# Key features of a polynomial-sketch attention: sums left in PSUM for the first factor, products from PSUM and SBUF by group of tiles

## The chip, the cores and the metric

The kernel runs on one core of one Trainium2 chip. The metric is device time in microseconds (us), the median of repeated runs; 425.93 us before the change. A profile of one execution gives the times of the single instructions. The engines are TensorE (PE, with its weight loads as PEld), VectorE (DVE), ScalarE (ACT), GpSimd (POOL) and SyncE (SP, which issues DMAs).

## What is computed

Two blocks one after the other. The first is an attention without softmax. Each query and key vector is projected twice, and the outer product of the two projections is its feature vector; the second is a sum over four experts, each a two-layer MLP. Cut to what matters:

```python
def phi(x):                                  # x: (4, 4, 1088, 32), S1, S2: (8, 32)
    a = np.einsum('rd,bhsd->bhsr', S1, x)    # first factor, 8 numbers
    b = np.einsum('rd,bhsd->bhsr', S2, x)    # second factor, 8 numbers
    return np.einsum('bhsi,bhsj->bhsij', a, b).reshape(*x.shape[:-1], 64)
q_p, k_p = (phi(q), phi(k))
kv = np.einsum('bhsf,bhsd->bhfd', k_p, v)
z = np.sum(k_p, axis=2)
num = np.einsum('bhsf,bhfd->bhsd', q_p, kv)
den = np.einsum('bhsf,bhf->bhs', q_p, z)[..., None] + 1e-06
x = (num / den)                              # laid out as 4352 tokens of 128
p = domain_probs / (domain_probs.sum(-1, keepdims=True) + 1e-09)
for e in range(4):                           # w1: (4, 128, 1024), w2: (4, 1024, 128)
    out += p[:, e:e + 1] * (np.maximum(x @ w1[e], 0.0) @ w2[e])
```

S1 and S2 come as float64. The kernel writes each of their numbers as a float32 and a smaller rest, so a projection is a product with the high part plus a product with the low part.

## The kernel before

**The main loop.** The MLP takes the tokens in ten chunks of 128 to 512 and, for each chunk and expert, the hidden units in eight blocks of 128. One pass of the loop at line 1468 is one such block (a slot; the first chunk, of 128 tokens, takes two blocks a slot). A block of the usual kind (`opening`, line 1094) takes one PSUM bank `g`, and PE multiplies two of three weight parts into it (`h<-xs,wa` and `h<-xs,wb`); ACT scales the bank in place (L1135). One slot later `third` (line 1154) adds the third part (`h<-xs,wd`) and has the engines make three operands out of the bank: ACT `ha` (L1184) and for some blocks `hc` (L1186), DVE `hb` (L1191) and for some `hc` (L1206), POOL others (L1213, L1214). Some slots later `second` (line 1220) multiplies these by the second layer (`o<-ha,va`, `o<-hb,vb`, `o<-hc,vd`). So each block of this kind has one `wa` matmul and one `hb`, and both come in the order of the blocks. `MAKERS` says by a letter which engine makes what for each block.

**The banks.** Six of the eight PSUM banks serve the tag `h`. Their owner is decided when the program is written out, by a queue (lines 123 to 137): `psum` takes the bank at the head of `spare`, `given_back` puts one at its tail. A block's bank is given back in `third`, that is one slot after it was taken. A matmul into a bank waits on the chip until the last reader of the bank's previous content has finished.

**The attention as pieces.** The attention of batches 1 to 3 is written as generators (`keys`, `queries`), and each `yield` ends a piece. The loop deals the pieces among the slots (`work`, line 1483): a credit grows by a rate that follows how many pieces the next chunk still needs, and a piece is written out while there is credit and the estimated DVE time `vector_time` is under `LIMIT` (1300 ns). `on_vector` (line 1407) adds elements/0.96 + 80 ns for each DVE instruction, and each slot takes off 1600 ns for a chunk of 512 tokens (1400 for 448). Batch 0 goes another way (`start`, line 966), which the change leaves alone.

**The keys of one batch.** 1088 keys of four heads are nine tiles of 128 (the last is half full), in groups of 4, 4 and 1 (`FG`, line 449). The tile `kp` holds the transposed keys (from its column 1024) and later the features. In `keys` (line 562):

- three pieces transpose the keys on DVE;
- `key_project_wide` (line 491) takes a bank `kf`, makes one matmul per tile, 128 columns each (64 of the high part of S, then 64 of the low part; each 64 are 4 heads by 16, 8 first factors and 8 second), and ACT copies the high half into the SBUF tile `fs` (this copy has L51 in the profile, the helper's line);
- `key_add` (line 504) adds the low half, from PSUM, to `fs`, on DVE, in place; the bank is given back, before the next group takes its own;
- `key_product_wide` (line 519) multiplies first and second factors out of `fs`, both operands in SBUF, into `kp`: four instructions, tiles 0 to 3 and 4 to 8, for each of two pairs of heads (p), with an empty piece after each;
- the queries are turned, and 80 small matmuls (L318) sum the features times the values and project the queries.

Up to the turn of the queries that makes three pieces of transposes, three of projections (the last two with an add) and eight of products, the first of which has the third add.

Of the kernel before, what the change touches and what calls it, by code (L numbers as in the profile page):

```python
# [12 lines left out]
ALU = mybir.AluOpType  # L13
# [4 lines left out]
def _ap(t, p0: int, np_: int, off: int, free):  # L18

    p = list(t.ap)[0]  # L20
    return bass.AP(t.tensor, t.offset + p0 * p[0] + off, [[p[0], np_]] + [list(d) for d in free])
# [3 lines left out]
def kernel(  # L25
# [24 lines left out]
    nc = tc.nc  # L50
    scalar_copy = lambda to, of: nc.scalar.activation(to, of, ACTF.Copy)  # L51

    P = 128
    HP = 64
    B, H, S, D = q.shape
    E, DM, F = w1.shape
    R = 8
    R2 = 2 * R
    G = S // 32
    assert (B, H, S, D) == (4, 4, 1088, 32) and (E, DM, F) == (4, P, 1024)  # L60
    NT = 9
# [56 lines left out]
    ps_h = ctx.enter_context(tc.tile_pool(name="ps_h", bufs=1, space=bass.MemoryType.PSUM))  # L118
# [6 lines left out]
    def psum(pool, tag):  # L125
        if pool is not ps_h:
            return pool.tile([P, 512], F32, tag=tag, name=tag)
        bank = spare.pop(0)
        t = pool.tile([P, 512], F32, tag=f"h{bank}", name="h")
        home[t.tensor.name] = bank  # L130
        return t

    def given_back(t):

        bank = home.pop(t.tensor.name, None)
        if bank is not None:
            spare.append(bank)
# [12 lines left out]
    def load_q(b):  # L150
        qn[b] = lpool.tile([P, S], F32, tag="rows", name="qn")
        load_rows(q, b, qn[b])
# [104 lines left out]
    sk = cpool.tile([P, P], F32, name="sk")  # L257
# [5 lines left out]
    kTs, kps = {}, {}  # L263

    def key_tiles(b):
        t = apool.tile([P, NT * 2 * P], F32, tag="kp", name="kp")
        kps[b] = t[:, :].rearrange("p (t i f) -> p t i f", i=2, f=P)
        kTs[b] = t[:, NT * P - P :]
        nc.gpsimd.memset(kTs[b][:, S : P * NT], 0.0)
# [179 lines left out]
    FG = ((0, 4), (4, 4), (8, 1))  # L449
    fss, kvzs, kvx = {}, {}, {}  # L450

    def key_turn(b, r, t0=0, n=4):
        if r < 2:
            nc.vector.transpose(
                _ap(kTs[b], 0, P, 512 * r + P * t0, [[P, n], [32, 4], [1, 32]]),
                _ap(kn[b], 0, P, P * r + 32 * t0, [[32, n], [8 * D, 4], [1, 32]]),
            )
        else:
            nc.vector.transpose(kTs[b][:, 1024:S], kn[b][:, 1024:S])

    def value_copy(b):
        if b:
            return
        for r in range(2):
            scalar_copy(
                vx[:, 4 * r : 4 * r + 4, :, 0:D].rearrange("p t h d -> p h t d"),
                _ap(vn[b][r], 0, P, 0, [[4 * D, H], [D, 4], [1, D]]),
            )
            yield
        scalar_copy(vx[0:64, 8, :, 0:D], _ap(vn[b][2], 0, 64, 0, [[D, H], [1, D]]))  # L470
# [20 lines left out]
    def key_project_wide(b, gi, kf):  # L491

        t0, n = FG[gi]
        if gi == 0:
            fss[b] = apool.tile([P, 2, NT, 32], F32, tag="fs", name="fs")
        for t in range(n):
            nc.tensor.matmul(  # L497
                kf[:, P * t : P * t + P], kTs[b][:, P * (t0 + t) : P * (t0 + t + 1)], sk[:, :], start=True, stop=True
            )
        scalar_copy(  # L500
            _ap(fss[b], 0, P, 32 * t0, [[32 * NT, 2], [32, n], [1, 32]]), _ap(kf, 0, P, 0, [[32, 2], [P, n], [1, 32]])
        )

    def key_add(b, gi, kf):
        t0, n = FG[gi]
        fs = _ap(fss[b], 0, P, 32 * t0, [[32 * NT, 2], [32, n], [1, 32]])
        nc.vector.tensor_tensor(out=fs, in0=_ap(kf, 0, P, HP, [[32, 2], [P, n], [1, 32]]), in1=fs, op=ALU.add)

    def key_product(b, t0, n, p, x, eng, kf=None):

# [5 lines left out]
            op=ALU.mult,  # L516
        )

    def key_product_wide(b, t0, n, p):

        nc.vector.tensor_tensor(
            out=_ap(kps[b], 0, P, 256 * t0 + P * p, [[256, n], [HP, 2], [1, HP]]),
            in0=_ap(fss[b], 0, P, 32 * (NT * p + t0), [[32, n], [R2, 2], [1, R], [0, R]]),
            in1=_ap(fss[b], 0, P, 32 * (NT * p + t0) + R, [[32, n], [R2, 2], [0, R], [1, R]]),
            op=ALU.mult,
        )

    def key_sum(b, p, kv, t0=0, n=NT):
        for t in range(t0, t0 + n):
            both(  # L530
                kv[:, 256 * p : 256 * p + 2 * (D + 1)],
                kps[b][:, t, p, :],
                vx[:, t, 2 * p : 2 * p + 2].rearrange("p h d -> p (h d)"),

                start=(p == t == 0),
                stop=(t == NT - 1),
                skip_group_check=True,
            )
# [13 lines left out]
    def key_blocks(b, kv):  # L552

        kvx[b] = apool.tile([P, 2, 2 * (D + 1)], F32, tag="kvx", name="kvx")
        nc.vector.tensor_tensor(
            out=_ap(kvx[b], 0, P, 0, [[2 * (D + 1), 2], [D + 1, 2], [1, D + 1]]),
            in0=_ap(kv, 0, P, 0, [[256, 2], [D + 1, 2], [1, D + 1]]),
            in1=_ap(own_half if b else own2, 0, P, 0, [[0, 2], [1, 2], [0, D + 1]]),
            op=ALU.mult,
        )  # L560

    def keys(b):
        key_tiles(b)
        for r in range(3):
            key_turn(b, r)
            yield
        load_q(b)
        kf = []
        for gi in range(3):
            if gi:  # L570
                key_add(b, gi - 1, kf[gi - 1])
                given_back(kf[gi - 1])
            kf.append(psum(ps_h, "h") if gi == 1 else psum(ps_h, "h"))
            key_project_wide(b, gi, kf[gi])
            yield
        key_add(b, 2, kf[2])
        given_back(kf[2])
        for _ in value_copy(b):
            yield
        for t0, n in ((0, 4), (4, 5)):  # L580
            for p in range(2):
                key_product_wide(b, t0, n, p)
                yield
                yield
        first = UNITS[b][0]
        turned[b, 0] = query_turn(b, 0, first)
        yield
        yield
        kv = psum(ps_h, "h")
        for p in range(2):  # L590
            key_sum(b, p, kv)
        project(b, 0, first)
        yield
        key_blocks(b, kv)
        given_back(kv)
        yield
        store_rows(b, 0, first)
        if SPREAD:
            spread(b, 0, first)
        yield  # L600
# [29 lines left out]
    def query_turn(b, c, n):  # L630
        qT = apool.tile([P, QW], F32, tag="qT", name="qT")
        for _ in query_turns(b, c, n, qT):
            pass
        return qT
# [140 lines left out]
    def project(b, c, n):  # L775

        qT = turned[b, c]
        qc, w = psum(ps_h, "h"), n // 2
        for i in range(2):
            for _ in range(2):  # L780
                on_side(
                    lambda s: qc[half[s], 0:w],
                    lambda s: sq_half[:, i, :],
                    lambda s: qT[:, w * s : w * s + w],
                    start=(i == 0),
                    stop=(i == 1),
                )
        scalar_copy(qT[:, 0:w], qc[:, 0:w])
        given_back(qc)
# [3 lines left out]
    def store_rows(b, c, n):  # L793

        qT, w = turned.pop((b, c)), n // 2
        rows = rows_of_unit[b, c] = dram.tile([HP, n], F32, name=f"rows_{b}_{c}")
        for s in range(2):
            nc.sync.dma_start(rows[:, w * s : w * s + w], qT[half[s], 0:w])
        if SPREAD == 0:
            spread(b, c, n)  # L800

    def spread(b, c, n):

        rows = rows_of_unit.pop((b, c))
        t = fetched[b, c] = apool.tile([P, 4, QW], F32, tag="kp", name="qs")
        for p in range(2):
            at = rows.offset + R2 * p * n
            nc.sync.dma_start(t[:, p, 0:n], bass.AP(rows.tensor, at, [[n, R2], [0, R], [1, n]]))
            for i in range(2):
                nc.sync.dma_start(  # L810
                    t[half[i], 2 + p, 0:n], bass.AP(rows.tensor, at + (32 + R * i) * n, [[0, R], [n, R], [1, n]])
                )
# [220 lines left out]
    def front():  # L1033
        for b in range(B):
            if b:
                yield from keys(b)
                if b + 1 < B:
                    load_v(b + 1)
            c = 0
            for n in UNITS[b]:  # L1040
                if b or c:
                    yield from queries(b, c, n)
                c += n
# [424 lines left out]
    while i < len(slots) or i <= max(due) or owed:  # L1468
        vector_time[0] = max(0.0, vector_time[0] - (SLOT * CHUNKS[slots[i][1]] / CW if i >= first_slot[1] and i < len(slots) else 900.0))
        scalar_time[0] = max(0.0, scalar_time[0] - (SLOT_A * CHUNKS[slots[i][1]] / CW if i >= first_slot[1] and i < len(slots) else 900.0))  # L1470
        if i < len(slots):
            kind, m, _, _ = slots[i]
# [101 lines left out]
```

## Time and profile before

| | |
|---|---|
| three runs | 425.80, 425.93, 425.94 us |
| median | 425.93 us |
| the profiled execution, its own time | 426.43 us |
| its span from first to last instruction | 424.7 us |
| granted TensorE clock | 1.00 |
| DVE busy in 54 to 60, 70 to 76 us | 5.97, 5.90 of 6 us |
| ACT busy in 148 to 154, 154 to 160 us | 6.00, 4.46 of 6 us |
| key projections (L497), three batches | 54 matmuls, 272/275/275 ns |
| ACT copies into `fs`, all batches | 12, 211/384/477 ns |

Triples are shortest, median and longest. In a row of a profile, `kp<-fs` is what is written and what is read, by the program's names; `x12` is a count; an entry in brackets is the time that the engine stood idle before the row, and what ended it. A row's duration runs from its start to its end, and rows of one engine overlap a little. L numbers are lines of the kernel. "Busy" counts the time in which at least one instruction was under way.

### The profile page before, as it was taken

To read this page: it belongs to the slowest core of one execution; us is meant where nothing else is said; L and a number is where in the kernel's file an instruction comes from. 1 tells how busy PE (TensorE), PEld (TensorE's weight loads), DVE (VectorE), ACT (ScalarE), POOL (GpSimd) and SP (SyncE) were. 2 spreads that over 40 slices of the span, in tenths; PEclk is the share of its full clock that TensorE was granted. 3 is DMA by queue.
4 is the path that set the end of the run, shared out by engine and by line. 5 is a ranking of instruction groups with operands and counts; after the bars stand their busy time and mean duration, and the time that the engine had idled before them with its cause. 6 is when DMAs were issued, how large, how long until landed. Compare 5 with 4: busy or idle time off the path is not lost.

```text
span 424.7 us, 8812 instructions
## 1 busy us (share of the span) xinstructions
PE 416.5 (98%) x2819; PEld 351.7 (83%) x2819; DVE 357.0 (84%) x626; ACT 382.0 (90%) x818; POOL 355.3 (84%) x371
## 2 busy tenths in 40 slices
PE   9999999999999999999999999999999999999996
PEld 7886677888888887878888887878778888989995
DVE  5869999888798896898799996896897878879894
ACT  4368898999999998999999988998999999999992
POOL 6441468999999999997999998897989999799992
PEclk9999999999999999999999999999999999999999
DMA  6925250446512401643602415212621221040110
GB/s 194 320 60 130 47 145 2 98 80 158 165 40 51 126 27 44 136 99 95 176 5 61 114 26 117 61 33 62 161 32 23 41 75 35 23 82 27 34 38 19
DMA packets 57646, 34.66 MB, mean 82 GB/s; under 512 B 34945, under 2 KB 50689, under 8 KB 57601
## 3 DMA queue, kind: packets, MB, share of 16 engines
q1 hardware_dynamic: 57504, 34.01, 31.5%
q8 instruction: 22, 0.36, 0.4%
q14 instruction: 24, 0.19, 0.2%
q10 hardware_dynamic: 96, 0.10, 0.1%
HBM read 28.94 MB, written 5.15 MB: 80 GB/s over the span
## 4 chain that ended last, share of the span: by engine, by line
PE 82%; ACT 8%; DVE 4%; issue 3%; DMA 2%; SPq 0%; DVEq 0%; ACTq 0%
PE o L949 36%; PE h L949 36%; PE h L318 6%; ACT ha L1184 3%; ACT h L1135 3%; ACT hc L1186 2%; PE h L497 1%; DMA qn_first<-in_q_dram 1%; PE o L318 1%; DMA kn<-in_k_dram 1%; PE h L1121 1%; DVE hb L1191 1%; DVE o L1396 1%; SPq L171 0%; DVE qs L637 0%
## 5 line engine op out<-in xcount | busy, mean ns | idle before, releaser
L1214 POOL TENSOR_TENSOR hc<-hb,hc 128x512 fp32r<-128x512 f32 (+3 forms) x204 | 252.5, 1260 | 23.1 <-DVE hb L1191 16.9
L1191 DVE SCALAR_TENSOR_TENSOR hb<-h,ha 128x512 fp32r<-128x512 f32 (+3 forms) x266 | 166.8, 641 | 48.9 <-ACT hc L1186 16.9
L1135 ACT ACTIVATE h<-h 128x512 f32<-128x512 f32 (+3 forms) x283 | 166.3, 588 | 4.1 <-PE h L949 3.5
L1184 ACT ACTIVATE ha<-h 128x512 fp32r<-128x512 f32 (+3 forms) x252 | 148.8, 590 | 2.0 <-PE h L949 0.4
L949 PE MATMUL h<-xs,wd 128*128 128x512 f32 (+3 forms) x283 | 109.2, 386 | 1.3 <-ACT h L1135 0.5
L949 PE MATMUL h<-xs,wa 128*128 128x512 f32 (+3 forms) x283 | 105.5, 373 | 0.0
L949 PE MATMUL h<-xs,wb 128*128 128x512 f32 (+3 forms) x283 | 102.5, 362 | 0.0
L949 PE MATMUL o<-ha,va 128*128 128x512 f32 (+3 forms) x266 | 96.8, 364 | 1.1 <-DVE total L1397 1.1
L949 PE MATMUL o<-hb,vb 128*128 128x512 f32 (+3 forms) x266 | 96.6, 363 | 0.0
L949 PE MATMUL o<-hc,vd 128*128 128x512 f32 (+3 forms) x262 | 79.7, 366 | 0.2
L1186 ACT ACTIVATE hc<-h 128x512 fp32r<-128x512 f32 (+3 forms) x124 | 74.1, 598 | 0.0
L949 PEld LDWEIGHTS h<-xs,wd 128*128 128x128 f32 x283 | 53.3, 188 | 19.8 <-ACT h L1135 11.6
L1213 POOL TENSOR_SCALAR hc<-ha 128x512 fp32r<-128x512 f32 (+3 forms) x80 | 57.4, 717 | 8.1 <-ACT ha L1184 1.6
L949 PEld LDWEIGHTS h<-xs,wa 128*128 128x128 f32 x283 | 53.5, 189 | 9.5 <-issue 2.9
L949 PEld LDWEIGHTS h<-xs,wb 128*128 128x128 f32 x283 | 53.5, 189 | 5.7 <-issue 0.6
L949 PEld LDWEIGHTS o<-ha,va 128*128 128x128 f32 x266 | 50.3, 189 | 7.5 <-PE h L949 2.3
L949 PEld LDWEIGHTS o<-hc,vd 128*128 128x128 f32 x262 | 48.5, 189 | 7.9 <-issue 1.6
L949 PEld LDWEIGHTS o<-hb,vb 128*128 128x128 f32 x266 | 50.3, 189 | 5.5 <-DVE hb L1191 0.2
L1193 DVE SCALAR_TENSOR_TENSOR hc<-ha,hb 128x512 fp32r<-128x512 f32 (+2 forms) x41 | 36.2, 882 | 1.4
L1268 ACT ACTIVATE o<-o 128x512 f32<-128x512 f32 (+3 forms) x33 | 18.4, 557 | 0.0
L1397 DVE TENSOR_TENSOR total<-o,total 128x512 f32<-128x512 f32 (+3 forms) x26 | 16.9, 650 | 0.9
L1396 DVE TENSOR_TENSOR o<-o,gate 128x512 f32<-128x512 f32 (+3 forms) x26 | 16.8, 647 | 0.3 <-PE o L949 0.3
(161 smaller groups left out, 405.2 us busy)
## 6 DMA issues: line engine op xcount, KB each, us to landing
w_sb<-in_moe_w_dram SPq DMA_DIRECT2D x8, 512.0 KB
gate<-gates SPq DMA_DIRECT2D x16, 256.0 KB
kn<-in_k_dram SPq DMA_DIRECT2D x4, 544.0 KB
gate<-gates SPq DMA_DIRECT2D x8, 224.0 KB
qs<-rows SPq DMA_DIRECT2D x6, 288.0 KB
qs<-rows SPq DMA_DIRECT2D x12, 144.0 KB
qn<-in_q_dram SPq DMA_DIRECT2D x3, 544.0 KB
vx<-in_v_dram SPq DMA_DIRECT2D x48, 32.0 KB
```

What stands on the lines that cost most here:

```text
L318: nc.tensor.matmul(out(s), weights(s), moving(s), **flags)
L949: nc.tensor.matmul(to, weights, t, **flags)
L1135: nc.scalar.activation(g, g, ACTF.Copy, scale=1.0 + R12)
L1184: nc.scalar.activation(ha, g, ACTF.Relu, scale=NEAR)
L1186: nc.scalar.activation(hc, g, ACTF.Relu, scale=NEAR * R12)
L1191: nc.vector.scalar_tensor_tensor(out=hb, in0=g, scalar=0.0, in1=high, op0=ALU.max, op1=ALU.subtract)
L1193: nc.vector.scalar_tensor_tensor(out=hc, in0=high, scalar=-R12, in1=rest, op0=ALU.mult, op1=ALU.add)
L1213: nc.gpsimd.tensor_scalar(out=hc, in0=high, scalar1=R12, scalar2=1.0, op0=ALU.mult, op1=ALU.mult)
L1214: nc.gpsimd.tensor_tensor(out=hc, in0=rest, in1=both_, op=ALU.subtract)
L1268: nc.scalar.activation(o[:, 0:n], o[:, 0:n], ACTF.Copy, scale=1.0 + R12)
L1396: nc.vector.tensor_tensor(out=o[:, 0:n], in0=o[:, 0:n], in1=g, op=ALU.mult)
L1397: nc.vector.tensor_tensor(out=total[m][:, 0:n], in0=o[:, 0:n], in1=total[m][:, 0:n], op=ALU.add)
```

## The change

The matmul of the key projection writes its 128 columns as four strips of 32, one for each half of S and pair of heads, so that the bank holds the group by strip, then tile. The ACT copy of the high half follows that layout. `key_add` becomes two instructions of half the size: the first factors' sum is written back into the bank, the second factors' sum into `fs` as before. `key_product_wide` takes a group in place of a range of tiles and reads the first factor from the bank and the second from `fs`: six instructions a batch, for groups of 4, 4 and 1 tiles. In `keys`, the next group's bank is taken and its projection written out ahead of the add of the group before; that group's two products follow in pieces of their own, and its bank is given back after the second. The first product of a group is a piece after its add. The number of pieces up to the turn of the queries stays: three of transposes and eleven behind them.

```diff
--- before.py
+++ after.py
@@ -495,16 +495,24 @@
             fss[b] = apool.tile([P, 2, NT, 32], F32, tag="fs", name="fs")
         for t in range(n):
             nc.tensor.matmul(
-                kf[:, P * t : P * t + P], kTs[b][:, P * (t0 + t) : P * (t0 + t + 1)], sk[:, :], start=True, stop=True
+                _ap(kf, 0, P, 32 * t, [[P, 4], [1, 32]]),
+                kTs[b][:, P * (t0 + t) : P * (t0 + t + 1)],
+                sk[:, :].rearrange("p (a c) -> p a c", c=32),
+                start=True,
+                stop=True,
             )
         scalar_copy(
-            _ap(fss[b], 0, P, 32 * t0, [[32 * NT, 2], [32, n], [1, 32]]), _ap(kf, 0, P, 0, [[32, 2], [P, n], [1, 32]])
+            _ap(fss[b], 0, P, 32 * t0, [[32 * NT, 2], [1, 32 * n]]), _ap(kf, 0, P, 0, [[P, 2], [1, 32 * n]])
         )
 
     def key_add(b, gi, kf):
         t0, n = FG[gi]
-        fs = _ap(fss[b], 0, P, 32 * t0, [[32 * NT, 2], [32, n], [1, 32]])
-        nc.vector.tensor_tensor(out=fs, in0=_ap(kf, 0, P, HP, [[32, 2], [P, n], [1, 32]]), in1=fs, op=ALU.add)
+        of_fs, of_kf = [[32 * NT, 2], [R2, 2 * n], [1, R]], [[P, 2], [R2, 2 * n], [1, R]]
+        nc.vector.tensor_tensor(
+            out=_ap(kf, 0, P, 0, of_kf), in0=_ap(kf, 0, P, 2 * P, of_kf), in1=_ap(fss[b], 0, P, 32 * t0, of_fs), op=ALU.add
+        )
+        fs = _ap(fss[b], 0, P, 32 * t0 + R, of_fs)
+        nc.vector.tensor_tensor(out=fs, in0=_ap(kf, 0, P, 2 * P + R, of_kf), in1=fs, op=ALU.add)
 
     def key_product(b, t0, n, p, x, eng, kf=None):
 
@@ -516,11 +524,12 @@
             op=ALU.mult,
         )
 
-    def key_product_wide(b, t0, n, p):
-
+    def key_product_wide(b, gi, kf, p):
+
+        t0, n = FG[gi]
         nc.vector.tensor_tensor(
             out=_ap(kps[b], 0, P, 256 * t0 + P * p, [[256, n], [HP, 2], [1, HP]]),
-            in0=_ap(fss[b], 0, P, 32 * (NT * p + t0), [[32, n], [R2, 2], [1, R], [0, R]]),
+            in0=_ap(kf, 0, P, P * p, [[32, n], [R2, 2], [1, R], [0, R]]),
             in1=_ap(fss[b], 0, P, 32 * (NT * p + t0) + R, [[32, n], [R2, 2], [0, R], [1, R]]),
             op=ALU.mult,
         )
@@ -567,21 +576,25 @@
         load_q(b)
         kf = []
         for gi in range(3):
+            kf.append(psum(ps_h, "h"))
+            key_project_wide(b, gi, kf[gi])
             if gi:
                 key_add(b, gi - 1, kf[gi - 1])
-                given_back(kf[gi - 1])
-            kf.append(psum(ps_h, "h") if gi == 1 else psum(ps_h, "h"))
-            key_project_wide(b, gi, kf[gi])
+                yield
+                for p in range(2):
+                    key_product_wide(b, gi - 1, kf[gi - 1], p)
+                    if p:
+                        given_back(kf[gi - 1])
+                    yield
+            else:
+                yield
+        key_add(b, 2, kf[2])
+        yield
+        for p in range(2):
+            key_product_wide(b, 2, kf[2], p)
+        given_back(kf[2])
+        for _ in range(3):
             yield
-        key_add(b, 2, kf[2])
-        given_back(kf[2])
-        for _ in value_copy(b):
-            yield
-        for t0, n in ((0, 4), (4, 5)):
-            for p in range(2):
-                key_product_wide(b, t0, n, p)
-                yield
-                yield
         first = UNITS[b][0]
         turned[b, 0] = query_turn(b, 0, first)
         yield
```

`value_copy` yields nothing for the batches that come this way.

## What was predicted

> **What bounds the kernel now.** I read the page's busy times and chain first, then the chain of waits in order of time and the busy times by stretch around the three places where the changed code runs, then the DVE groups by shape, and last the rows in order of time.
>
> ```profile
> PE 416.5 (98%) x2819; PEld 351.7 (83%) x2819; DVE 357.0 (84%) x626; ACT 382.0 (90%) x818; POOL 355.3 (84%) x371
> PE 82%; ACT 8%; DVE 4%; issue 3%; DMA 2%; SPq 0%; DVEq 0%; ACTq 0%
> ```
>
> TensorE (PE) holds 82% of the chain that ended last. VectorE (DVE) is busy 84% of the span but has 4% of that chain. What a DVE saving is worth is therefore decided in the three stretches where `keys` runs (batch 1 near 55 to 70 us, batch 2 near 139 to 156, batch 3 near 232 to 250):
>
> ```profile
> core 0: us, PE busy (x) PEld busy (x) DVE busy (x) ACT busy (x) POOL busy (x), PEclk, DMA share, GB/s
> 60.00:70.00 10.00, 9.31 (x44) 7.37 (x42) 9.89 (x16) 9.93 (x22) 9.33 (x8) 1.00 0.10 23
> 142.00:148.00 6.00, 6.00 (x31) 5.28 (x30) 4.17 (x9) 5.71 (x13) 5.67 (x6) 1.00 0.53 137
> 236.00:242.00 6.00, 6.00 (x31) 5.28 (x30) 5.25 (x10) 5.97 (x13) 5.43 (x6) 1.00 0.73 177
> ```
>
> In batches 2 and 3 PE has no gap, and in the chain by time its matmuls follow at 0.215 us each from 132 to 166 us and from 226 to 260 us. Nothing can be gained there. Every wait that PE is given is added to the end. In batch 1, from 60.1 to 69.8 us, the chain runs through ScalarE (ACT) and "issue"; ACT is busy 9.93 of 10 us and DVE 9.89.
>
> **Part 1, the DVE work.** The durations:
>
> ```profile
> L521 DVE TENSOR_TENSOR kp<-fs 128x640 f32<-128x640 f32 x6 | 7.1, 1191 | 0.0
> L521 DVE TENSOR_TENSOR kp<-fs 128x512 f32<-128x512 f32 x6 | 5.7, 949 | 0.0
> L507 DVE TENSOR_TENSOR fs<-h,fs 128x256 f32<-128x256 f32 x6 | 2.5, 412 | 0.0
> L507 DVE TENSOR_TENSOR fs<-h,fs 128x64 f32<-128x64 f32 x3 | 0.7, 218 | 0.0
> L1396 DVE TENSOR_TENSOR o<-o,gate 128x512 f32<-128x512 f32 x18 | 12.4, 687 | 0.0
> L726 DVE TENSOR_TENSOR xs<-h,rc 128x128 f32<-128x128 f32 x5 | 1.4, 280 | 0.0
> ...
> L521 DVE TENSOR_TENSOR kp<-fs x12: 681/998/1802, 59.4 to 248.8; 128x512 f32<-128x512 f32 x6, 128x640 f32<-128x640 f32 x6
> ```
>
> The old product (two SBUF operands) takes anything from 681 to 1802 ns. The operations with one PSUM operand hardly spread. The new product of four tiles is 512 elements, one PSUM and one SBUF operand: 687 ns by L1396. That of one tile is 128 elements: 280 ns by L726. The repeated operand costs nothing extra: L512 in the first batch has the same pattern and gives 419 ns for 256 elements against L507's 412. The sums are split in two of half the size. From L507's two rows, (412-218)/192 = 1.01 ns an element, so 128 elements are 283 ns and 32 are 186 ns. Writing the sum to PSUM is not dearer: L1396 writes PSUM too.
>
> Per batch, before: adds 2x0.412+0.218 = 1.04 us, products 2x0.949+2x1.191 = 4.28, together 5.32 us in 7 instructions. After: adds 4x0.283+2x0.186 = 1.50, products 4x0.687+2x0.280 = 3.31, together 4.81 us in 12. That is 0.5 us less a batch, 1.5 us less in all. Bounds: if no old product had been held up (0.68 and 0.81 us, the least seen of each shape) the old sum would be 4.0 and the new one costs 0.8 more a batch; if all were like the worst, 2.5 us less. I take the means. On the end this is worth 0 in batches 2 and 3, since PE is the chain there, and I take 0 in batch 1, since ACT is. The cover in batch 1 is thin, and what it is worth if it is gone is the rival on the fast side.
>
> [...]
>
> **Part 2, the key projection and its copy.** Each of the 54 matmuls of L497 (275 ns) writes four strips of 32 columns in place of 128 in a row. In the first batch the projection already writes strips of 32, and the sums of products write 66 columns in a row:
>
> ```profile
> L318 PE MATMUL h<-vx,kp x288: 220/222/272, 9.3 to 254.5; 128*64 128x66 f32 x144
> L318 PE MATMUL h<-sk,kp x72: 222/222/334, 5.8 to 8.0; 128*64 128x64 f32 x72
> ```
>
> Both have 222 ns, so 0. The ACT copy moves as many elements in longer runs: 0, covered on ACT in batches 2 and 3 by PE being the chain. The third group's projection (0.22 us of PE in the chain) and its copy (0.22 us of ACT) move some blocks later. In batch 1 that takes 0.22 us out of a stretch that PE sets (to 59.8 us) and puts the copy into the one that ACT sets: net 0.
>
> **Part 3, the planner.** Per batch `vector_time` now sees 2x427 + 2x(613+613) + 227 + 427 = 3960 ns, where it saw 347+347+147+613+613+747+747 = 3561 (elements/0.96 plus 80 each). Against `LIMIT` I find no piece of batches 2 and 3 pushed to another block: the old products start at 145.74, 148.57, 151.77 and 154.96 us, one in two blocks of some 1.5 us, as their two yields say, so one piece runs in a block and the new ones do too. In batch 1 the third piece reaches 740+613 = 1353, over 1300, and the following four run one to three blocks late. Nothing waits for them before the sums of products at 72.4 us. No DMA is issued elsewhere.
>
> **Part 4, the banks.** This is what I expect to decide. The six `h` banks go round in a queue, and a block of the MLP takes one. With no other user a block reopens the bank of the sixth block before it; each bank that the keys hold shortens that by one. Before, a key bank was back at the next piece. Now group 0's is held over three pieces, group 1's is taken while it is out, and group 2's while group 1's is. At one place in each batch a block then gets the bank of the third block before it. Its first matmul (`h<-xs,wa`) must wait for the last reader of that bank, VectorE's `hb` or `hc`. One `wa` and one `hb` row belong to each block, in the same order, which gives these pairs:
>
> ```profile
> 145.00 0.69 DVE L1191 SCALAR_TENSOR_TENSOR hb<-h,ha 128x512 fp32r<-128x512 f32 x1 [0.97 <-ACT hc L1186]
> 145.35 0.38 PE L949 MATMUL h<-xs,wa 128*128 128x512 f32 x1
> ...
> 238.81 0.68 DVE L1206 SCALAR_TENSOR_TENSOR hc<-h,hid 128x512 fp32r<-128x512 f32 x1
> 238.95 0.38 PE L949 MATMUL h<-xs,wa 128*128 128x512 f32 x1
> ...
> 61.76 0.35 PE L949 MATMUL h<-xs,wa 128*128 128x448 f32 x1
> 62.34 1.26 DVE L1191 SCALAR_TENSOR_TENSOR hb<-h,ha 128x448 fp32r<-128x448 f32 x2
> 62.83 0.55 ACT L1135 ACTIVATE h<-h 128x448 f32<-128x448 f32 x1
> ```
>
> Batch 2: the reader ends at 145.69, the matmul began at 145.35; 0.34 us, and 0.05 for the signal (an L1135 ends at 54.86 and the weight load that it frees starts at 54.91): 0.39 us. This reader waited for ACT, so no lighter DVE brings it forward. Batch 3: 239.49 less 238.95, 0.54, plus 0.07 for DVE having one product more ahead and 0.05: 0.66 us. Batch 1: the first of the two `hb` ends at 62.97, 1.21 us after 61.76; DVE has two adds less ahead of it by then and may end 0.4 sooner, so PE waits 0.8. PE was ahead of ACT there: its second matmul, over at 62.30, would be over at 63.10, and ACT wanted it at 62.83. 0.3 us of that shows. The block after each takes group 0's own bank, free soon after its second product, and the others have 0.4 to 2 us left: 0. What is queued behind the waiting matmul is all of PE; ACT waits next.
>
> Bounds: 0 for each, if the reader comes earlier by as much as PE waits; 0.7 (batch 2, hit at two blocks), 1.2 (batch 3, likewise) and 1.2 (batch 1, all of it) on the other side. I take 0.39 + 0.66 + 0.3 = 1.35 us.
>
> **Sum.** The profiled execution has 426.43 us for its span of 424.7, 1.73 around it; 424.7 + 1.35 + 1.73 = 427.78. It lies 0.50 above the median, 425.93, which is what I count from: 425.93 + 1.35 = **427.3 us**, for this case alone 426.6 to 428.2.
>
> **Rivals.** I call 0.2%, 0.85 us, the least that a measurement of this kernel tells from no change: 426.8 and 425.1 are the borders.
>
> *The waits vanish* (chance 0.26): the readers come some tenths earlier because no product of 1.2 to 1.8 us stands in DVE's queue. For it: batch 2's wait is only 0.39, and DVE idles 0.97 us just before. Against: that reader and batch 3's come before the first long product. Half the waits or less, 426.2 us.
>
> *Faster, the one on the other side* (0.12): in batch 1 it is DVE, not ACT, that sets 60 to 70 us. Its products there took 0.68, 1.27, 0.81 and 1.80 us, with 1.05 of adds 5.61; the new set is 4.81, and twelve rows overlapping by 0.06 each in place of seven (59.36 to 59.96 for a row of 0.68) give 0.3 more: 1.1 us, and 424.8. It decides if the waits of that stretch end on DVE (idle 0.11 of its 10 us) and not on ACT (idle 0.07); the chain names ACT, which speaks against.
>
> *Dependencies* (0.10): ACT's copy of a later group into `fs` waits for the products that still read `fs`, or the third projection waits for products into `kp`, which lie in the same tile. About 1 us a batch on top of the banks: 430.0. Against: in the first batch projections start at 5.8 us while the last transpose into `kp` starts at 6.5, so parts of a tile are told apart.
>
> *Strips cost* (0.02): if four strips doubled the key matmuls, 2.0 us of PE a batch in the chain would be added three times: 425.9 + 1.35 + 6.0 = 433.3. Both 222 ns rows speak against. [...]
>
> **The numbers.** 0.50 for the forecast, 0.26, 0.12, 0.10 and 0.02 for the rivals. Slower by over 0.2%: nearly all of the forecast and the last two, 0.60; within: 0.28; faster: 0.12. The range, 425.2 to 429.2, leaves out most of the fast case and of the dependencies.
>
> **What would show it.** The key products are 12 rows near 690 and 6 near 280 ns with no spread, the adds 12 rows near 0.28 us and 6 near 0.19. In the waits PE gains entries for `wa` behind DVE `hb` or `hc`, one or two a batch, 0.3 to 0.8 us each, and batches 2 and 3 reach their sums of products 0.4 and 1.05 us later, counted from the stretch before. If no such waits appear the bank step is wrong; if they do and the end does not move, the claim that PE is the chain there is.

## The result, and the profile after

| | before | after |
|---|---|---|
| median of four runs each | 425.94 us (425.80 to 426.58) | 428.25 us (428.11 to 428.67) |
| the profiled execution, its own time | 426.43 us | 428.38 us |
| its span | 424.7 us | 426.6 us |

The ratio is 1.0054, with a 95% interval of 1.0041 to 1.0067: the changed kernel is 2.3 us slower. The forecast was 427.3 us, 1.35 us slower. The traces of experiments 1 and 3 below come from executions at a lower granted clock (0.56 and 0.85), so their times are not read, and such executions are left out of the medians of the experiments. All lines below `key_add` have moved; the main loop's matmuls (L949 before) are L962, `hb` (L1191) is L1204, `hc` on DVE (L1206) is L1219, the key product (L521) is L530 and the sums are L511 (first factors) and L515 (second). Each experiment's kernel has line numbers of its own; go there by the names of the tiles.

The page of after, with busy times and shares of the chain that ended last:

```profile
PE 417.4 (98%) x2819; PEld 352.1 (83%) x2819; DVE 356.4 (84%) x641; ACT 382.0 (90%) x818; POOL 349.6 (82%) x371
PE 84%; ACT 7%; DVE 4%; issue 2%; DMA 1%; POOL 1%; SPq 0%; DVEq 0%; ACTq 0%
```

DVE has 15 instructions more and 0.6 us less to do, and PE holds a larger part of a longer chain. The busy times by stretch (columns as shown of before):

```profile
60.00:70.00 10.00, 8.88 (x43) 7.14 (x41) 9.71 (x22) 9.36 (x22) 8.57 (x9) 1.00 0.07 25
94.00:98.00 4.00, 3.85 (x54) 2.39 (x52) 3.64 (x6) 2.81 (x6) 3.83 (x4) 1.00 0.13 18
142.00:148.00 6.00, 5.99 (x30) 5.13 (x29) 5.23 (x11) 5.75 (x14) 5.66 (x6) 1.00 0.53 139
236.00:242.00 6.00, 5.49 (x27) 4.67 (x26) 5.93 (x12) 5.26 (x11) 5.30 (x5) 1.00 0.68 176
```

PE, which had no gap from 236 to 242 us, now stands idle for 0.51 us of it; from 94 to 98 us, where before it was busy for 4.00 of 4 us, it stands idle for 0.15. The second of these stretches was not in the prediction.

PE's waits, in the list of what each engine waited for (total us, times, longest), have two lines for a block's `wa` that before has not:

```profile
PE h L962 <- DVE hb L1204: 1.1, 2, 0.7
PE h L962 <- DVE hc L1219: 0.5, 1, 0.5
```

The rows in order of time show the waits: the reader of the bank on DVE, then the matmul that reopens the bank (in batch 2 its weight load, which waits in its place), with the idle time in brackets. Two are in batch 1, one each in batches 2 and 3. Each tile of the key projection shows as two rows of L497 (54 rows for 27 tiles):

```profile
61.90 1.33 DVE L1204 SCALAR_TENSOR_TENSOR hb<-h,ha 128x448 fp32r<-128x448 f32 x2
62.67 0.43 PE L962 MATMUL h<-xs,wa 128*128 128x448 f32 x1 [0.73 <-DVE hb L1204]
...
64.99 0.62 DVE L1204 SCALAR_TENSOR_TENSOR hb<-h,ha 128x448 fp32r<-128x448 f32 x1
65.76 0.44 PE L962 MATMUL h<-xs,wa 128*128 128x448 f32 x1 [0.32 <-DVE hb L1204]
...
145.71 0.69 DVE L1204 SCALAR_TENSOR_TENSOR hb<-h,ha 128x512 fp32r<-128x512 f32 x1 [0.36 <-POOL hc L1227]
146.06 0.39 PE L497 MATMUL h<-sk,kp 128*128 128x128 f32 x2
146.46 0.19 PEld L962 LDWEIGHTS h<-xs,wa 128*128 128x128 f32 x1 [0.20 <-DVE hb L1204]
...
238.85 0.68 DVE L530 TENSOR_TENSOR kp<-h,fs 128x512 f32<-128x512 f32 x1
239.45 0.68 DVE L1204 SCALAR_TENSOR_TENSOR hb<-h,ha 128x512 fp32r<-128x512 f32 x1
240.05 0.68 DVE L1219 SCALAR_TENSOR_TENSOR hc<-h,hid 128x512 fp32r<-128x512 f32 x1
240.79 0.48 PE L962 MATMUL h<-xs,wa 128*128 128x512 f32 x1 [0.51 <-DVE hc L1219]
```

The waits of 0.73, 0.20 and 0.51 us are where the prediction put them, behind the readers that it named. The one of 0.32 us was not predicted: that block reopens the bank of the fourth block before it.

To see what reaches the end I set the start of every block's `wa` in one trace against its start in the other. A step in the difference is time lost or gained at that block:

| start of the block's `wa`, before | after | difference |
|---|---|---|
| 34.52 us | 34.40 us | -0.12 |
| 76.74 (batch 1's keys are done) | 77.04 | +0.30 |
| 92.41 | 92.69 | +0.28 |
| 98.46 | 99.40 | +0.94 |
| 146.86 (in batch 2's keys) | 148.07 | +1.21 |
| 240.46 (in batch 3's keys) | 242.40 | +1.94 |
| 298.22 | 300.17 | +1.95 |

So four places lose: batch 1's keys 0.42 us, a place between 92 and 98 us 0.66, batch 2's keys 0.27 and batch 3's 0.73. Together that is 2.1 us. The chain in order of time, before and then after, shows the place that the prediction had not named (start, duration, link):

```profile
93.44 0.22 PE h L949
93.66 2.18 PE h L318 x48
95.84 0.63 PE h L949 x2
```

```profile
94.14 0.68 ACT h L1148
94.82 0.04 issue
94.86 0.48 PE h L962
95.35 0.09 issue
95.44 0.45 PE o L962
95.89 2.18 PE h L318 x48
```

The 48 small matmuls of batch 1's queries (features times the sums over the keys, and the next projection) ran ahead of the block that began at 95.77 us before; now they run behind it. Without these 2.18 us of work in between, PE reached the blocks' other matmuls before ACT and POOL had delivered, and waited: starts 94.42, 94.86, 95.44 and 95.82 us, where the five from 93.56 to 94.42 us follow each other by 0.21 to 0.22. The weight loads of the last three show idle times of 0.47 us (ended by ACT's `h`, L1148), 0.36 (no releaser in the profile) and 0.23 (ended by POOL's `hc`, L1227). PE lost 0.75 us in these three steps.

### The profile page after: what moved, and what is told of

It reads as the page before. It is cut to its first block, busy times and chain, and to the rows that moved or that the text cites. A ratio compares the mean times of both kernels' runs of the same rounds, so it can differ in the third digit from the quotient of the medians.

```text
span 426.6 us, 8832 instructions
## 1 busy us (share of the span) xinstructions
PE 417.4 (98%) x2819; PEld 352.1 (83%) x2819; DVE 356.4 (84%) x641; ACT 382.0 (90%) x818; POOL 349.6 (82%) x371
## 4 chain that ended last, share of the span: by engine, by line
PE 84%; ACT 7%; DVE 4%; issue 2%; DMA 1%; POOL 1%; SPq 0%; DVEq 0%; ACTq 0%
PE o L962 35%; PE h L962 35%; PE h L318 8%; ACT ha L1197 3%; ACT h L1148 2%; PE o L318 2%; DVE hb L1204 2%; ACT hc L1199 1%; PE h L497 1%; DMA qs<-rows 1%; PE h L304 1%; PE h L1134 1%; DVE o L1409 1%; DVE hc L1206 0%; DVE total L1410 0%
## 5 line engine op out<-in xcount | busy, mean ns | idle before, releaser
L1227 POOL TENSOR_TENSOR hc<-hb,hc 128x512 fp32r<-128x512 f32 (+3 forms) x204 | 249.1, 1242 | 30.4 <-DVE hb L1204 23.5
L1204 DVE SCALAR_TENSOR_TENSOR hb<-h,ha 128x512 fp32r<-128x512 f32 (+3 forms) x266 | 167.0, 641 | 49.9 <-ACT hc L1199 17.0
L1148 ACT ACTIVATE h<-h 128x512 f32<-128x512 f32 (+3 forms) x283 | 166.8, 589 | 5.1 <-PE h L962 4.6
L962 PE MATMUL h<-xs,wd 128*128 128x512 f32 (+3 forms) x283 | 109.0, 385 | 1.0 <-ACT h L1148 0.2
L962 PE MATMUL h<-xs,wa 128*128 128x512 f32 (+3 forms) x283 | 105.7, 374 | 1.6 <-DVE hb L1204 1.1
L962 PE MATMUL h<-xs,wb 128*128 128x512 f32 (+3 forms) x283 | 102.5, 362 | 0.0
L962 PE MATMUL o<-ha,va 128*128 128x512 f32 (+3 forms) x266 | 96.8, 364 | 1.1 <-DVE total L1410 1.1
L962 PE MATMUL o<-hb,vb 128*128 128x512 f32 (+3 forms) x266 | 96.5, 363 | 0.0
L962 PE MATMUL o<-hc,vd 128*128 128x512 f32 (+3 forms) x262 | 79.7, 367 | 0.3
L962 PEld LDWEIGHTS h<-xs,wd 128*128 128x128 f32 x283 | 53.3, 188 | 18.8 <-ACT h L1148 10.8
L962 PEld LDWEIGHTS h<-xs,wa 128*128 128x128 f32 x283 | 53.5, 189 | 12.1 <-issue 3.6
L1226 POOL TENSOR_SCALAR hc<-ha 128x512 fp32r<-128x512 f32 (+3 forms) x80 | 55.0, 687 | 8.8 <-ACT ha L1197 2.3
L962 PEld LDWEIGHTS h<-xs,wb 128*128 128x128 f32 x283 | 53.5, 189 | 5.8 <-issue 0.6
L962 PEld LDWEIGHTS o<-ha,va 128*128 128x128 f32 x266 | 50.3, 189 | 7.5 <-PE h L962 2.3
L962 PEld LDWEIGHTS o<-hc,vd 128*128 128x128 f32 x262 | 48.5, 189 | 8.2 <-issue 2.0
L962 PEld LDWEIGHTS o<-hb,vb 128*128 128x128 f32 x266 | 50.3, 189 | 5.4 <-DVE hb L1204 0.2
L1206 DVE SCALAR_TENSOR_TENSOR hc<-ha,hb 128x512 fp32r<-128x512 f32 (+2 forms) x41 | 37.0, 903 | 1.4
```

Of the source, the lines that this page charges most:

```text
L962: nc.tensor.matmul(to, weights, t, **flags)
L1148: nc.scalar.activation(g, g, ACTF.Copy, scale=1.0 + R12)
L1204: nc.vector.scalar_tensor_tensor(out=hb, in0=g, scalar=0.0, in1=high, op0=ALU.max, op1=ALU.subtract)
L1206: nc.vector.scalar_tensor_tensor(out=hc, in0=high, scalar=-R12, in1=rest, op0=ALU.mult, op1=ALU.add)
L1226: nc.gpsimd.tensor_scalar(out=hc, in0=high, scalar1=R12, scalar2=1.0, op0=ALU.mult, op1=ALU.mult)
L1227: nc.gpsimd.tensor_tensor(out=hc, in0=rest, in1=both_, op=ALU.subtract)
```

## The experiments

All with the time of before on the same chip beside them. The ratio is to that, with its 95% interval. The theory was that banks held over several blocks cost what was lost. The rival was that the new instructions or the new order of the work do.

**1. The old work with the banks held.** The old layout, sum and SBUF products, but by group, in the new order of pieces, and each bank given back as late as in the changed kernel.

```diff
+                for p in range(2):
+                    key_product_wide(b, *FG[gi - 1], p)
+                    if p:
+                        given_back(kf[gi - 1])
+                    yield
```

> The old adds and old products (both operands in fs, by group of 4, 4 and 1 tiles) in the new order of pieces, with the banks held as long as the new kernel holds them. Bank theory: the waits of wa in batches 2 and 3 come back at the same blocks (0.4 and 0.8 us), batch 1 gives 0 to 0.5, so 427.1 to 427.7 us. Rival (the new DVE instructions cost it: split adds, PSUM as operand and target): 425.7 to 426.2.

429.70 us (median of four) against 426.11, ratio 1.0084 (1.0069 to 1.0098): slower, as the bank theory has it, but by 2 us more than it allowed.

**2. The same, with the bank given back right after the sum.**

```diff
             if gi:
                 key_add(b, gi - 1, kf[gi - 1])
+                given_back(kf[gi - 1])
                 yield
                 for p in range(2):
                     key_product_wide(b, *FG[gi - 1], p)
-                    if p:
-                        given_back(kf[gi - 1])
                     yield
```

> As the one before, but each key bank is given back right after its add, as the old kernel does. It differs from it in nothing but that. Bank theory: no wa waits in batches 2 and 3, 425.6 to 426.3 us. Rival (the order of the pieces, with the next group projected ahead of the add and products spread over single blocks): the same time as the run with the banks held, 427 us or more.

427.83 us, ratio 1.0043 (1.0029 to 1.0057). The two differ only in when the bank comes back, and by 1.9 us: holding it has a cost of its own. But the expected time was missed by over 1 us. The difference of the starts grows by 1.28 us in batch 1 here. PE still waits for banks there, twice and behind `hb`:

```profile
PE h L952 <- DVE hb L1194: 1.7, 2, 1.2
```

Giving back right after the sum does not free batch 1, since in the new order of pieces the sums of the second and third groups come three pieces after their projection, where before each came one piece after. Both waits are for the fourth block before. The old products of four tiles, now one a block in neighbouring blocks, also keep DVE from `hb`; in this kernel they take up to 1621 ns. In batches 2 and 3 no `wa` waits behind `hb` or `hc`.

**3. One bank at a time.** The new layout, sums and products, but a group is projected only after the bank of the group before is back.

```diff
         for gi in range(3):
+            kf = psum(ps_h, "h")
+            key_project_wide(b, gi, kf)
+            yield
+            key_add(b, gi, kf)
+            yield
+            key_product_wide(b, gi, kf, 0)
+            if gi < 2:
+                yield
+            key_product_wide(b, gi, kf, 1)
+            given_back(kf)
```

> The new adds and products, but each group is projected only after the products of the group before have given its bank back, so one key bank is out at a time; as many pieces, the same DVE instructions. Bank theory: batches 2 and 3 lose their wa waits (1.3 us less than the new kernel); what is left is batch 1 and what follows it, so 426.4 to 427.1 us. Rival (DVE work): as the new kernel, 428.0 to 428.5.

426.78 us, ratio 1.0017 (1.0005 to 1.0030). Two thirds of the loss are gone with the new instructions all in place. The pieces of batch 1 come as late as in the changed kernel: the 48 matmuls of its queries stand behind the block here too.

**4. The planner's estimates put back.** The changed kernel, where each piece of `keys` adds to `vector_time` what the piece at that place added before, so that the pieces of batch 1 fall in their old blocks.

```diff
+        was = [0.0, 347.0, 347.0, 760.0, 0.0, 613.0, 0.0, 747.0, 0.0, 747.0, 0.0]
+        def as_before():
+            vector_time[0] = seen[0] + was[step[0]]
+            step[0] += 1
```

> The new kernel, with the planner given the old kernel's DVE estimate for each piece, so that every piece falls into the block that it had before. Bank theory with the planner's shift as a second, smaller cost: the waits in batches 2 and 3 stay, the 0.5 us lost at 94 to 96 us in the new kernel goes and batch 1 loses less, so 427.0 to 427.6 us. Rival (the shift of pieces is the whole cost): 425.8 to 426.2.

428.25 us, ratio 1.0052 (1.0040 to 1.0065): no gain, a miss for the whole. The trace says why. The loss between 92 and 98 us is gone (-0.02 in place of 0.64), so the planner's shift did cause it. But batch 2 now loses 0.82 in place of 0.28, as `hb` comes later there against PE: it starts 0.17 us after the key projection's matmul, in the changed kernel 0.35 us before it.

```profile
144.97 0.68 DVE L530 TENSOR_TENSOR kp<-h,fs 128x512 f32<-128x512 f32 x1
145.40 0.38 PE L497 MATMUL h<-sk,kp 128*128 128x128 f32 x2
145.57 0.68 DVE L1221 SCALAR_TENSOR_TENSOR hb<-h,ha 128x512 fp32r<-128x512 f32 x1
146.31 0.48 PE L979 MATMUL h<-xs,wa 128*128 128x512 f32 x1 [0.52 <-DVE hb L1221]
```

The wait is 0.52 us where the changed kernel has 0.20.

**5 and 6. The change in batch 1 alone, and in batches 2 and 3 alone.** Both codes side by side, chosen by `b == 1` and by `b > 1`.

> The new code for batch 1 alone, the old code for batches 2 and 3. From the trace of the changed kernel: bank waits in batch 1, 0.6 us, and a later bank wait at 94 to 96 us, because the planner put the pieces behind it one block later, 0.5 us. Bank theory with the planner: before + 0.8 to 1.4 us, and the wait at 94 to 96 us is there. Rival (batch 1 is bound by ACT and DVE, so its lighter DVE pays for the waits and batches 2 and 3 make the whole loss): before + 0 to 0.4.

> The old code for batch 1, the new code for batches 2 and 3. Bank theory: waits of wa of 0.4 and 0.9 us at 145 and 239 us, before + 1.0 to 1.5 us. Together with the run of batch 1 alone it should add up to the whole change, some 2.2 us. Rival (batch 1 decides): before + 0 to 0.4.

427.41 and 427.31 us against 426.32, ratios 1.0021 (1.0011 to 1.0031) and 1.0022 (1.0013 to 1.0031). The two losses, 1.09 and 0.99 us, add up to 2.08 of the whole change's 2.3, within its interval. Batch 1's part has the 0.64 us between 92 and 98 us in it, batches 2 and 3 have not.

**7. One bank at a time in batches 2 and 3 alone, batch 1 as before.**

> The old code for batch 1; for batches 2 and 3 the new products and adds, with one key bank out at a time. No block gets a bank from fewer than four blocks back. Bank theory, and that a lighter DVE is worth nothing where PE has no gap: before, within 0.3 us. Rival (new DVE work costs in itself, or helps): more than 0.6 us above or below.

426.25 us, ratio 1.0002 (0.9989 to 1.0014). With the same new DVE work as in experiment 6 the loss is gone, and no `wa` waits behind `hb` or `hc`. The sums and projections also come in another order than in experiment 6, so this pair alone does not single out the bank; that the waits are for a bank is in their rows, and experiments 2 and 10, which differ in the give-back alone, show it too. The lighter products gain nothing here.

**8. Before with the layout alone**: the strips of the matmul, the copy and the sum that follow them, one sum and SBUF products as before.

> The old kernel with nothing but the new layout of the projection: four strips of 32 columns, the ACT copy and the single add of 256 elements following it. Both bank and DVE theory: before, within 0.3 us, L497's matmuls at 275 ns as they were. Rival (strips slow the matmuls or the copies): up to 6 us slower, and the durations show it.

426.04 us, ratio 0.9995 (0.9986 to 1.0004).

**9. Experiment 3 with the planner's estimates put back in batch 1**, to have both losses out.

> The new adds and products, one key bank out at a time, and the planner given the old estimates in batch 1, so that the pieces fall where they fell before the change. If the cost of the change is the banks held together (some 1.4 to 1.6 us) plus the products of values moved one block later near 94 to 97 us (0.5 us), both are gone here: 426.1 to 426.6 us, within 0.2% of before, no wait of wa behind hb or hc near 145 and 239 us, and the blocks near 94 to 97 us start as before. If something in the new DVE work itself costs, 427 or more is left. If the lighter DVE work in batch 1 is worth something once nothing else is lost, 425.0 to 425.6.

426.87 us against 426.02, ratio 1.0020 (1.0011 to 1.0029): a miss. The loss between 92 and 98 us and the waits of batches 2 and 3 are gone, but batch 1 still has two waits, the second of them longer:

```profile
62.78 0.43 PE L973 MATMUL h<-xs,wa 128*128 128x448 f32 x1 [0.73 <-DVE hb L1215]
65.75 0.45 PE L973 MATMUL h<-xs,wa 128*128 128x448 f32 x1 [0.84 <-DVE hb L1215]
```

A further 0.4 us is lost at the first blocks of the next chunk, near 122 us, where DVE comes 0.7 us later to the block's `hb`.

**10. Experiment 1 once more, for its trace.**

> The same kernel as the first experiment, for the rows of its trace. If the 2 us between holding and giving back with the old products are waits for the bank, PE has waits of wa behind hb or hc near 145 and 239 us that the kernel with the banks given back does not have, together near 1 to 2 us, at the same two blocks as in the changed kernel. If there are none, the 2 us come from elsewhere.

429.03 us in the one run. The waits are there, at the expected two blocks (0.20 us in batch 2, in the weight load). In batch 3:

```profile
238.86 1.32 DVE L521 TENSOR_TENSOR kp<-fs 128x512 f32<-128x512 f32 x1
240.10 0.68 DVE L1195 SCALAR_TENSOR_TENSOR hb<-h,ha 128x512 fp32r<-128x512 f32 x1
240.70 0.67 DVE L1210 SCALAR_TENSOR_TENSOR hc<-h,hid 128x512 fp32r<-128x512 f32 x1
241.43 0.48 PE L953 MATMUL h<-xs,wa 128*128 128x512 f32 x1 [1.15 <-DVE hc L1210]
```

These four rows stand against the last four of after, above. The product ahead of the reader takes 1.32 in place of 0.68 us, 0.64 more, and the wait is 1.15 in place of 0.51, 0.64 more. So the lighter product does have a price on the path, but only where a held bank puts it there.

**11. Experiment 9 with a group projected, added and multiplied within one block in batch 1**, so that its bank is back before the next block takes one.

```diff
+            key_add(b, gi, kf)
+            if b > 1:
+                yield
+            key_product_wide(b, gi, kf, 0)
+            if b > 1 and gi < 2:
+                yield
+            key_product_wide(b, gi, kf, 1)
+            given_back(kf)
```

> As the experiment before with one bank at a time and the old places of the pieces, but in batch 1 a group is projected, added and multiplied within one block, so its bank goes back before the next block takes one. Only one block of batch 1 then takes the bank of the fourth block before it (0.6 us short by the times of before), none two. If the bank waits of 0.73 and 0.84 us are what batch 1 still cost, at most one of them is left: 425.8 to 426.4 us, no slower than before. If batch 1 costs by its new DVE instructions, whatever the banks: 426.8 or more, as without this edit. If lighter DVE work gains once the banks are out of the way: 425.0 to 425.6, faster than before.

427.14 us against 426.35, ratio 1.0017 (1.0008 to 1.0026): a miss again. One bank wait of 0.7 us is left, as expected, and in place of the other PE waits 0.3 us for a product (L530) and, at a projection, 0.3 us for `hb`. DVE is busy 9.76 of the 10 us from 60 to 70.

**The traces side by side.** What the difference of the `wa` starts to before grows by, from one place to the next (us; the places are near 34, 77, 121, 196 and 298 us):

| kernel | batch 1's keys | 77 to 121 | batch 2's keys | batch 3's keys | sum | ratio less 1, times 426 |
|---|---|---|---|---|---|---|
| the changed kernel | 0.43 | 0.64 | 0.28 | 0.72 | 2.07 | 2.3 |
| 2 old work, banks back early | 1.28 | -0.02 | 0.14 | 0.42 | 1.82 | 1.8 |
| 4 old estimates | 0.50 | -0.02 | 0.82 | 0.75 | 2.05 | 2.2 |
| 5 batch 1 alone | 0.44 | 0.64 | 0.00 | -0.04 | 1.04 | 0.9 |
| 6 batches 2, 3 alone | -0.01 | -0.03 | 0.28 | 0.72 | 0.96 | 0.9 |
| 7 the same, one bank | -0.01 | 0.00 | 0.05 | -0.04 | 0.00 | 0.1 |
| 8 layout alone | -0.02 | -0.03 | 0.01 | -0.04 | -0.08 | -0.2 |
| 9 one bank, old estimates | 0.52 | -0.02 | 0.42 | -0.02 | 0.90 | 0.9 |
| 10 old work, banks held | 1.27 | -0.02 | 0.42 | 1.38 | 3.05 | - |
| 11 within one block | 0.65 | -0.02 | 0.39 | -0.03 | 0.99 | 0.7 |

The sums of single traces and the measured ratios agree within 0.3 us in every row that has both. Row 10 has one run; the same kernel in experiment 1 lost 3.6 us (2.9 to 4.2). (The 0.42 and 0.39 of experiments 9 and 11 in batch 2's column are the loss near 122 us. In row 2, 0.13 of batch 2's 0.14 is lost there too, and batch 3's 0.42 between 246 and 252 us; at the blocks near 145 and 239 us that kernel loses nothing.)

Rows 2 and 10 tell where holding the banks costs, with the old products: nothing more in batch 1, 0.27 us at batch 2's blocks and 1.37 at batch 3's. With what each loses elsewhere, the two sums are 1.2 us apart, where the medians of experiments 1 and 2 are 1.9 apart. No version with batch 1's sums and products changed came out at the time of before, and none under it by more than the intervals.

## Why the prediction was right, and where it was not

**Part 1, the DVE work: right in its durations.** The groups by shape, of after:

```profile
L530 DVE TENSOR_TENSOR kp<-h,fs 128x512 f32<-128x512 f32 x12 | 8.2, 681 | 0.0
L515 DVE TENSOR_TENSOR fs<-h,fs 128x128 f32<-128x128 f32 x6 | 1.7, 291 | 0.2
L511 DVE TENSOR_TENSOR h<-h,fs 128x128 f32<-128x128 f32 x6 | 1.7, 289 | 0.0
L530 DVE TENSOR_TENSOR kp<-h,fs 128x128 f32<-128x128 f32 x6 | 1.4, 281 | 0.0
L530 DVE TENSOR_TENSOR kp<-h,fs x18: 273/681/684, 58.7 to 249.7; 128x512 f32<-128x512 f32 x12, 128x128 f32<-128x128 f32 x6
```

687 and 280 ns were predicted for the products, 283 for the sums; 681, 281 and 289 to 291 came, with no spread. Means times counts give 14.5 us for the key rows in place of 16.0: 1.5 less, as predicted. DVE's busy time fell by 0.6 only, since other rows took longer (`hc<-ha,hb` of 128x512 took 26.9 us in place of 25.9). With one operand in PSUM the 512-element product is no slower than the quickest of before with both in SBUF: 681 ns each. That the saving is worth nothing in batches 2 and 3 is shown by experiment 7, within 0.6 us. In batch 1 it is not shown: no version there was free of new waits.

**Part 2, strips and copy at nothing: right**, by experiment 8, and the L497 rows, which write strips of 32 columns after and 128 in a row before, have 272/275/348 ns after and 272/275/275 before (shortest, median, longest). The ACT copies into `fs` have 211/383/481 and 211/384/477 ns.

**Part 3, the planner: this step failed.** The shift was foreseen ("the following four run one to three blocks late"), and so was what shifted. "Nothing waits for them before the sums of products at 72.4 us" was wrong. I looked only at what consumes the late pieces. The pieces behind them in the same queue move too, and 20 us later the 48 matmuls of the queries changed sides with a block. That cost 0.64 us, predicted as 0; experiments 4 and 5 show that it comes from batch 1's estimates alone. It is most of the 0.9 us by which the forecast fell short.

**Part 4, the banks: right in mechanism and place**, and the largest term, as forecast. Experiments 1 and 2 (holding alone costs 1.9 us with the old work, 1.2 by the traces, all of it in batches 2 and 3) and 6 and 7 (one bank fewer out removes the loss) show it for batches 2 and 3. The sizes:

| term | predicted | in the trace |
|---|---|---|
| batch 1's keys | 0.30 | 0.43 |
| the queries' matmuls near 94 us | 0 | 0.64 |
| batch 2's keys | 0.39 | 0.28 |
| batch 3's keys | 0.66 | 0.72 |
| sum | 1.35 | 2.07 |

In batch 1 PE waits 0.73 us (0.8 predicted), but the other reuses were not all free, as "the others have 0.4 to 2 us left: 0" had it: the wait of 0.32 us at 65.76 comes on top. In batch 2 the two rows of the third group's projection (L497 at 146.06, 0.22 us of PE together) now stand in front of the waiting matmul and fill part of its wait; 0.20 of the 0.39 us is left. In batch 3 a new product at 238.85 us holds the reader up, and the same move of the projection hides part of that; that 0.66 and 0.72 lie so near is in part luck. In batches 2 and 3 the losses are larger than the waits in brackets (0.28 against 0.20, 0.72 against 0.51), among other things since the `wa` matmul after the wait takes 0.48 us in place of 0.38, which the sum did not have.

How much of batch 1's 0.43 us is the banks and how much the crowding of DVE stays open: experiments 9 and 11 changed both at once and lost 0.52 and 0.65. Experiment 3 speaks for the banks. It lost 0.7 us (0.2 to 1.3) in all, and if the changed place of the 48 matmuls cost it the 0.64 us that it cost the changed kernel, next to nothing is left for batch 1's keys; no trace of it shows that.

**The rivals.** "The waits vanish": they did not. With the difference that the `wa` starts had already taken off, the readers of batches 1 and 2 end 0.3 and 0.2 us sooner than before, which is not enough, and that of batch 3 no sooner. "Faster": batch 1's keys lose time in every changed version whose trace can be compared. "Dependencies": in the changed kernel no wait of ACT or of the projections is behind a key product (ACT's copies into `fs` wait 1.7 us for the matmuls of L318 and 0.3 for the projections), and DVE waits for a copy into `fs` in the first batch alone (1.0 us in three waits). "Strips cost": no.

## What to carry to other kernels

When an operand stays in a buffer that rotates among users, replay the rotation and ask of each reuse who reads the buffer last and when; here 1.5 us less in VectorE's key rows did not pay for 2.07 us lost on TensorE, which held 84% of the chain. When a change alters the numbers that a planner sees, replay the whole queue behind the change, past the last piece that was edited, and look for work on the bounding engine that changes places. Losses read block by block from two traces add up (here within 0.3 us), so that one table tells which part of a change to undo.

## What was not expected of the hardware

In the same order of pieces, the products of 512 and 128 elements took 277 to 1621 ns with both operands in SBUF (experiment 2) and 273 to 684 ns with one in PSUM. POOL gained as well, by the pages' busy times: 355.3 us before and 354.3 to 354.6 in the other kernels with the old products (experiments 2, 8, 10), 353.3 with the new products in one batch (5), 351.4 in two (6, 7) and 349.4 to 349.6 in three (the changed kernel, 4, 9, 11). The saving on both engines was real and steady, and no version shows it at the kernel's end.
